# VectorE's share of the softmax exponentials: four weighted bit readings instead of five

## The chip, the cores and the metric

The kernel runs on one core of a Trainium2 chip. The core's engines work side by side, each on its own instruction queue in order: TensorE (PE, matmuls; its weight loads are listed as PEld), VectorE (DVE), ScalarE (ACT), GpSimd (POOL) and SyncE (SP, which issues most DMAs). The metric is the device time of one execution in microseconds (us), as the median over runs.

## The reference

One transformer block with adaptive layer norm: 2048 tokens, width 512, 32 heads of 16, hidden width 1376.

```python
mod = (silu(c) @ w_mod).reshape(1, 6, 1, -1)      # sa, ca, ga, sb, cb, gb
h = layernorm(x) * (1 + ca) + sa
q, k, v = split(h @ wqkv)                          # 32 heads of 16
p = softmax(einsum('bhqd,bhkd->bhqk', q, k) * 16 ** -0.5)
x = x + ga * (einsum('bhqk,bhkd->bhqd', p, v) @ wo)
h = layernorm(x) * (1 + cb) + sb
x = x + gb * (gelu(h @ w1 + b1) @ w2 + b2)
```

## The kernel before

Attention is cut into 32 *runs*. A run is one block of 512 queries (`QB`) with four heads (in the last block: half the queries with eight heads), and passes over 16 key tiles of 128 keys (`NT`). A *unit* is 128 keys by 512 score columns; a run has 16 x 4 of them, the kernel 2048.

**Scores.** TensorE computes units by `qk` (L868). The four heads sit on four strips of 32 rows, so that several small score matmuls run side by side. For ScalarE, three and two units in turn go into one PSUM tile `st` (`SPAN = (3, 2)`); `qk_a` then issues one exp over 1536 or 1024 columns (L918), written as bf16 `pt`. For VectorE, units go one at a time into `ax`, a ring of two PSUM banks that all projections and the feed-forward part use too.

**Exponentials on VectorE.** Q is scaled so that a score plus a constant, rounded to a 16-bit integer, read as bf16 bits, is near the exponential; its error depends on the place within the mantissa. `qk_d` makes such readings `ph` (L966, one instruction of 128x512 per unit, four per key tile). Then `shifts` adds constants to the integers, which moves the reading to another place of the mantissa, and the sum over all readings evens the error out. The shifts are `PH_SH = (0, 24, 46, 70, 104)`:

- one shift of 128x2048 inside `ph` gives the second reading (L1019);
- one of 128x4096 from both readings into `sh` gives the third and fourth (L1019 again, out `sh`);
- the last, into `sl`, is made by `last_shift`: VectorE writes the first columns (L998), GpSimd the rest in parts of 128 32-bit words (256 columns, L1004) by adding the tile `step`. There are up to `PMAX` = 4 parts; `LIMIT` bounds how many may be outstanding.

**The sum with V.** `pv_op` (L1060) multiplies a tile of exponentials with V and accumulates into `od`: four matmuls of 512 columns side by side (eight of 256 in the last block). V lies in `VEB` with a column of ones per head, whose product is the softmax denominator. A key tile of ScalarE takes one such pass, one of VectorE five. `normalise` then copies `od` to `OD` (L1085), sends the denominators through DRAM, and GpSimd multiplies (L1112).

**What sets the order.** At build time a planner (`Plan`) lays out every instruction: each `op` has an engine, a duration, dependencies and a priority, buffers are `Res` rings, and the planner commits whichever can start first in its own clock. `SEEDS` mixes a small random term into the priorities, one number for each 12.5 us. `DKS` names the key tiles per run that VectorE may take (`d_job` decides whether there is time; the first run has only tile 14), and `next_tile` gives back to ScalarE those that VectorE did not reach. `after_dve` and the kind `beside` hold GpSimd's parts behind chosen VectorE instructions, and `in_turn` keeps the shifts of a run behind those of earlier runs. `heat` puts in zero matmuls (L444, L449, L460) where TensorE would idle long. `layer_norm` takes its statistics tile in the operation `ln`; `make_v` projects V and copies it from `ax` to `VEB`; `v_init` lets GpSimd set the ones and zeros of `VEB`. SyncE loads x by `load_x` and the weights in slices by `load_cols` (L527).

The feed-forward part and the output projections of earlier blocks are worked in between the runs; after the last exp, the second half of the last block remains.

Of the kernel before, what the change touches and what calls it, by code (L numbers as in the profile page):

```python
# [22 lines left out]

PH_SH = (0, 24, 46, 70, 104)
NPH = len(PH_SH)


def _gain():  # L30
    tot = 0.0
    for f in range(128):
        got = 0.0
        for sh in PH_SH:
            n, m = divmod(f + sh, 128)
            got += 2.0 ** n * (1 + m / 128)
        tot += math.log2(got) - f / 128
    return tot / 128

# [12 lines left out]
DL = 0.13  # L52
# [1 line left out]
AL = 0.31  # L54
FILL = 1.6
SPREAD = 0.3
SEEDS = (819, 778, 494, 247, 422, 169, 145, 549, 366, 204, 590, 973, 619, 101, 262, 478, 482, 0, 377, 943, 929, 5, 154, 378, 13, 70, 683, 7, 419, 919, 269, 223, 66, 0, 130, 0, 185, 0, 125, 986, 361, 514, 243, 995, 230, 969, 0, 765, 158, 613, 439, 598, 14, 562, 398, 933, 223, 842, 0, 0, 579, 0, 0, 0, 0, 0)
HEAT = 1.45


# [193 lines left out]
def kernel(  # L254
# [28 lines left out]
    EPS = 1e-5  # L283
    QSC = 0.25 * 128.0 / math.log(2.0)
    ESC = math.log(2.0) / 128.0
    DKS = (2, 6, 10, 14)
    WIDE = 1
    NPT = 4
    FEW = 1
# [26 lines left out]
    r_pt = [res(f"pt{n}_", NPT, [P, n * QB], BF16) for n in SPAN]  # L316
    r_ph = res("ph", 3, [P, 2 * 4 * QB], I16)
    r_sh = res("sh", 2, [P, 2 * 4 * QB], I16)
    r_s4 = res("sl", 2, [P, 4 * QB], I16)
    r_xb = res("xb", 2, [P, TPB, D], BF16)  # L320
    r_blk = res("blk", NQ, [P, NC, D], BF16)
    r_w = res("w", 3, [P, NC, D], BF16)
# [160 lines left out]
    b1_bf = const.tile([P, NF], BF16, name="b1_bf")  # L483
    b1c = const.tile([P, NF], FP32, name="b1c")
    VEB = [keep.tile([P, TPB, 32 * VW + 15], BF16, name=f"VEB{b}") for b in range(NQ)]
    kT = [[keep.tile([P, QB], BF16, name=f"kT{cc}_{b}") for b in range(NQ)] for cc in range(NC)]

    def v_tile(t):
# [64 lines left out]
    o_mask = op("DVE", mask, 0.6, (o_io,), prio=0.0)  # L553

    step = const.tile([P, STEP_N], I32, name="step")
    o_step = op("POOL", lambda o: nc.gpsimd.memset(step, PH_SH[-1] * 65537), 0.2, prio=0.3)

    o_v0 = {}

# [4 lines left out]
                mybir.DependencyClass.Sync, mybir.DependencyReason.DATA), reason="memsets behind the first norm")  # L564
            first_ln.append(got)

    def v_init(v, prio, gate, late):
        x = v[..., 0:32 * VW].rearrange("p t (h w) -> p t h w", w=VW)
        return [op("POOL", lambda o, to=to, c=c: fill(to, c, late), 0.35, prio=prio, gate=gate)
                for to, c in ((v[..., 32 * VW:32 * VW + 15], 0.0), (x[:, :, 8:32:8, 0:15], 0.0), (x[..., 16:17], 1.0))]  # L570

    first_ln = []
    for b in range(NQ):
        late = (lambda: True) if b == 0 else (lambda: first_ln)
        o_v0[b] = v_init(VEB[b], 1.0 + b, late, b > 0)

    o_ce = op("ACT", lambda o: nc.scalar.activation(out=ce, in_=c_bf, func=ACT.Tanh, scale=0.5),
              1.5, (o_c,), prio=0.0)
# [81 lines left out]
    def layer_norm(src, deps, mod, mod_dep, hold_z, alloc_h, engines, ps_res, kind, prio,  # L660
                   after=None, nt=TPB, by_part=False):

        ln = op("NIL", None, 0.0, (), lat=0.0, prio=0.0, acq=r_ln)
        st = [op("DVE", lambda o, t=t: stats(ln, t, src(t)), 0.83, (deps[t], ln, after and after[t]), prio=prio)
              for t in range(nt)]
        rs = [op("POOL", lambda o, i=i: rstd(ln, 2 * i, 2 * i + 2), 1.3,
# [127 lines left out]
    def make_v(b, cc, kind, acq, eng, after=None):  # L794
        def vt(ps, t):
            for j in range(NC):
                nc.tensor.matmul(out=ps[:, t * P:(t + 1) * P],
                                 lhsT=o_h[b].tile[:, j, t * P:(t + 1) * P],
                                 rhs=o_w[2].tile[:, j, cc * P:(cc + 1) * P],
                                 start=(j == 0), stop=(j == NC - 1))  # L800
        mm = chain([(lambda ps, t=t: vt(ps, t), 4 * 0.071) for t in range(TPB)],
                   [(o_w1 if cc else o_w0)[2], after] + o_hd[b], kind, acq, (o_h[b], o_w[2]))

        def ev(o):
            dst = VEB[b][:, :, 8 * cc * VW:8 * (cc + 1) * VW].rearrange(
                "p t (h w) -> p t h w", w=VW)
            copy(eng, dst[:, :, :, 0:16], mm.tile[:, 0:QB].rearrange("p (t h d) -> p t h d", t=TPB, h=8))
        got = [op(eng, ev, 0.6, [mm] + o_v0[b], prio=0.3, rel=(mm,))]
        o_v[(cc, b)] = got


# [119 lines left out]
    def qk_d():  # L931
        r, kts, rows = at["D"]
        if not rows:
            r, n = d_job()
            if n == 0:
                return
            kts = [shared[r].pop(0) for _ in range(n)]
            rows = [0, 1, 2, 3]
            at["D"][:] = r, kts, rows
            o_ph[0] = op("NIL", None, 0.0, (), lat=0.0, prio=0.0, acq=r_ph)  # L940
            o_ph[0].uses += 1
            d_e[:] = [[]]
        ph = o_ph[0]
        live["D"] += 1
        k = len(d_e) - 1
        kt = kts[k]
        deps, qm = qk_deps(r, kt)
        last = len(rows) == 1

        def go(o):  # L950
            n_d[0] += 1
            rows.remove(o.row)
            if last and k + 1 < len(kts):
                rows.extend((0, 1, 2, 3))
                d_e.append([])
            qk(o, 0, r, kt, o.row)
            live["D"] -= 1
        o = op("PE", go, MM, deps + [ph], lat=PEL, mode=("qk", rows[0]), kind="qkD", acq=r_ax, rel=(qm,),
               gate=lambda: n_d[0] - n_d[1] < 2)
        o.rows = list(rows)  # L960

        def ex(e):
            n_d[1] += 1
            units[0] += 1
            c0 = (4 * k + o.row) * QB
            nc.vector.tensor_scalar(out=ph.tile[:, c0:c0 + QB], in0=o.tile, scalar1=PH_B,  # L966
                                    scalar2=0.0, op0=ALU.add, op1=ALU.max)
        e = op("DVE", ex, 0.6, (o,), lat=DL, prio=0.5, rel=(o,))
        e.run = r
        d_e[k].append(e)  # L970
        if last:
            pv_op(r, kt, d_e[k], bits(ph, k), (ph,))
            if k + 1 == len(kts):
                shifts(r, kts, ph, [e for es in d_e for e in es])
                ph.uses -= 1
# [14 lines left out]
        sh.fn = go  # L990
        return sh

    def last_shift(r, kt, first, es, acq):
        into = in_turn(op("NIL", None, 0.0, es, lat=0.0, prio=0.0, acq=acq), r)
        n = max(0, min(PMAX, LIMIT - backlog[0]))
        w = 2 * STEP_N
        cols = 4 * QB - n * w
        parts = [in_turn(op("DVE", lambda o: nc.vector.tensor_scalar(  # L998
            out=into.tile[:, 0:cols], in0=first.tile[:, 0:cols], scalar1=PH_SH[-1], scalar2=None,
            op0=ALU.add), 0.06 + 0.54 * cols / (4 * QB), [into] + es, lat=DL, prio=2.0, rel=(first,), port=True), r)]  # L1000
        for i in range(n):
            def go(o, c=slice(cols + i * w, cols + (i + 1) * w)):
                backlog[0] -= 1
                after_dve(nc.gpsimd.tensor_tensor(  # L1004
                    out=into.tile[:, c].bitcast(I32), in0=first.tile[:, c].bitcast(I32), in1=step, op=ALU.add))
            backlog[0] += 1
            parts.append(op("POOL", go, POOL_US, [into, o_step] + es, lat=0.1, prio=0.6, kind="beside", rel=(first,),
                            port=True, gate=lambda: plan.beside(POOL_MIN)))
        pv_op(r, kt, parts, bits(into, 0), (into,))
    d_e = []  # L1010

    def bits(o, k):
        return lambda: [o.tile[:, h * QB:(h + 1) * QB].bitcast(BF16) for h in range(4 * k, 4 * k + 4)]

    def shifts(r, kts, first, es):
        kt, n = kts[0], 4 * QB

        def add(j, dst, src, us, deps, acq=None):
            o = op("DVE", lambda o: nc.vector.tensor_scalar(  # L1019
                out=dst(o), in0=src(), scalar1=PH_SH[j], scalar2=None, op0=ALU.add),  # L1020
                us, deps, lat=DL, prio=2.0, acq=acq, rel=(first,), port=True)
            return in_turn(o, r)
        one = op("NIL", None, 0.0, es, lat=0.0, prio=0.0)
        a = add(1, lambda o: first.tile[:, n:2 * n], lambda: first.tile[:, 0:n], 0.6, [one])
        b = add(2, lambda o: o.tile, lambda: first.tile, 1.14, [a], r_sh)
        first.uses += 1
        pv_op(r, kt, (a,), bits(first, 1), (first,))
        first.uses -= 1
        pv_op(r, kt, (b,), bits(b, 0), (b,))
        pv_op(r, kt, (b,), bits(b, 1), (b,))  # L1030
        last_shift(r, kt, first, [one], r_s4)

    def pv_op(r, kt, deps, srcs, owners):
        cc, par, hb = run_heads(r)

        def go(o):
# [18 lines left out]
            for n, p in enumerate(parts):  # L1055
                for i in range(4):
                    c0 = VW * (8 * cc + 2 * i + p)
                    w = QB if hb is None else HB
                    at = n * HB
                    nc.tensor.matmul(out=o_od[r].tile[32 * i:32 * i + 32, n * HB:n * HB + w],  # L1060
                                     lhsT=v_tile(kt)[:, c0:c0 + 32],
                                     rhs=got[i][:, at:at + w], start=first and hb is None,
                                     stop=(left[r] == 0 and p == parts[-1]), tile_position=(0, 32 * i))
            if o.extra:
# [510 lines left out]
```

## Time and profile before

| | |
|---|---|
| median of 3 runs | 777.62 us (777.03 to 778.87) |
| the profiled execution: span | 776.9 us |
| its own time beside the span | not listed apart; the runs lie 0.1 to 2.0 above the span, their median 0.7 |
| busy: ScalarE, TensorE, VectorE, GpSimd | 749.9, 729.5, 718.4, 281.7 us |
| first exp starts, last exp ends | 16.07, 752.72 us from the span's start |
| exps on ScalarE (L918) | 312 of 128x1536, 312 of 128x1024 |
| readings made by VectorE (L966) | 488, which is 122 key tiles |
| granted TensorE clock | 0.998 of full speed in the mean |

The span is the time from the first to the last instruction of one profiled execution. A row of a group gives line, engine, operation, output and input tiles with shapes, and the count; behind the first bar the busy time and the mean duration in ns of one; behind the second the engine's idle time just ahead of the group and what ended most of it. Neighbouring instructions of an engine overlap, so busy time is less than count times mean.

### The profile page before, as it was taken

Reading aid. Unit: us, or ns where it says so; the run is one execution under the profiler, and the core shown is the slowest. Engines: PE = TensorE matmul, PEld = TensorE weight load, DVE = VectorE, ACT = ScalarE, POOL = GpSimd, SP = SyncE. Lnnn points to the kernel's source line nnn. Section 1 sums busy time; section 2 is a strip of 40 time slices with the busy share of each in tenths; the row PEclk is TensorE's granted clock in tenths of the full one; section 3 lists DMA queues with packets and bytes.
Section 4 is the critical chain, followed back from the end, with each engine's and each line's share of the span. In section 5 each row is a group of like instructions: output and inputs, shape, how many; then the busy total and the mean of one; then the engine's idle time right before and its main releaser. Section 6 shows DMA issues by size and latency. Waiting matters only on the chain.

```text
span 776.9 us, 20734 instructions
## 1 busy us (share of the span) xinstructions
PE 729.5 (94%) x8318; PEld 274.2 (35%) x8318; DVE 718.4 (92%) x1196; ACT 749.9 (97%) x683; POOL 281.7 (36%) x624
## 2 busy tenths in 40 slices
PE   8889999999999999999998999999999999999998
PEld 3433333333333223223322333323243444344454
DVE  5858899999999999999999999999999999899984
ACT  3999999999999999999999999999999999999994
POOL 6124323444443434454444433333332333223320
PEclk9999999999999999999999999999999999999999
DMA  7034000100012010000100101000111000100100
GB/s 217 30 121 109 18 24 21 35 22 18 19 36 61 22 46 24 19 9 19 44 27 15 30 13 30 18 25 24 39 51 27 18 19 18 44 19 25 53 18 28
DMA packets 39075, 28.23 MB, mean 36 GB/s; under 512 B 17958, under 2 KB 34375, under 8 KB 38979
## 3 DMA queue, kind: packets, MB, share of 16 engines
q1 hardware_dynamic: 38970, 26.91, 12.4%
q8 instruction: 65, 1.06, 0.6%
q14 instruction: 32, 0.25, 0.1%
q10 hardware_dynamic: 8, 0.00, 0.0%
HBM read 21.30 MB, written 2.61 MB: 31 GB/s over the span
## 4 chain that ended last, share of the span: by engine, by line
ACT 53%; PE 24%; DVE 11%; issue 9%; DMA 1%; POOL 1%; SPq 0%; DVEq 0%; ACTq 0%
ACT pt L918 51%; PE od L1060 8%; PE st L868 6%; DVE ph L966 6%; PE ax L1283 2%; DVE sh L1019 1%; PE ax L868 1%; PE t L1227 1%; PE ax L747 1%; DVE ph L1019 1%; PE ax L1227 1%; DMA blk<-in_w_mod_dram 1%; PE t L1412 1%; DVE OD L1085 1%; ACT g L1298 1%
## 5 line engine op out<-in xcount | busy, mean ns | idle before, releaser
L918 ACT ACTIVATE pt<-st 128x1536 bf16<-128x1536 f32 x624 | 707.9, 1429 | 3.0 <-PE st L868 1.9
L966 DVE TENSOR_SCALAR ph<-ax 128x512 int16<-128x512 f32 x488 | 320.5, 682 | 18.6 <-PE ax L868 16.4
L1004 POOL TENSOR_TENSOR sl<-ph,step 128x128 int32<-128x128 int32 x361 | 166.2, 463 | 325.0 <-DVE sh L1019 95.8
L868 PE MATMUL st<-qm,kT 32*128 32x512 bf16 x1560 | 244.0, 382 | 32.0 <-ACT pt L918 25.7
L868 PEld LDWEIGHTS <-kT 32*128 32x128 bf16 x2048 | 86.4, 91 | 248.7 <-issue 238.2
L868 PE MATMUL ax<-qm,kT 32*128 32x512 bf16 x488 | 162.2, 381 | 3.1 <-DVE ph L966 2.4
L1060 PEld LDWEIGHTS <-VEB 128*32 128x32 bf16 x5024 | 109.1, 96 | 144.7 <-issue 120.4
L1019 DVE TENSOR_SCALAR sh<-ph 128x4096 int16<-128x4096 int16 x122 | 148.2, 1216 | 1.5 <-PE od L1060 1.4
L1060 PE MATMUL od<-pt,VEB 128*32 128x512 bf16 (+1 forms) x1944 | 147.2, 342 | 0.6 <-DVE OD L1085 0.4
L1060 PE MATMUL od<-ph,VEB 128*32 128x512 bf16 (+1 forms) x1232 | 91.2, 339 | 1.2 <-DVE OD L1085 0.6
L1060 PE MATMUL od<-sh,VEB 128*32 128x512 bf16 (+1 forms) x1232 | 86.8, 340 | 0.7 <-DVE sh L1019 0.6
L1019 DVE TENSOR_SCALAR ph<-ph 128x2048 int16<-128x2048 int16 x122 | 83.2, 685 | 0.4
L998 DVE TENSOR_SCALAR sl<-ph 128x1024 int16<-128x1024 int16 (+4 forms) x122 | 59.0, 488 | 0.7 <-PE od L1060 0.4
L1112 POOL TENSOR_TENSOR OT<-OD,RB 128x128 bf16<-128x128 f32 x76 | 34.3, 456 | 62.7 <-DVE sh L1019 27.0
L1060 PE MATMUL od<-sl,VEB 128*32 128x512 bf16 (+1 forms) x616 | 48.8, 339 | 0.3 <-POOL sl L1004 0.3
L1283 PE MATMUL ax<-blk,W 128*128 128x512 bf16 (+1 forms) x176 | 43.8, 356 | 0.7 <-DVE g L1287 0.4
L1112 POOL TENSOR_TENSOR OS<-OD,RB 128x128 bf16<-128x128 f32 x48 | 21.8, 456 | 40.3 <-DVE sh L1019 14.8
L747 PE MATMUL ax<-blk,w 128*128 128x512 bf16 x116 | 33.4, 382 | 1.0 <-DMA w<-in_A_wqkv_dram 0.7
L1227 PE MATMUL ax<-w,g 128*128 128x512 bf16 x96 | 26.6, 383 | 0.0
L1287 DVE TENSOR_SCALAR g<-ax,b1c 128x512 bf16<-128x512 f32 x33 | 24.4, 743 | 1.2 <-PE ax L1283 1.2
L627 DVE BATCH_NORM_STATS2 ln_s<-xb 128x6 f32<-128x512 bf16 x32 | 21.6, 674 | 3.4 <-DMA xb<-in_A_x_dram 3.3
L1085 DVE COPY OD<-od 128x512 f32<-128x512 f32 x31 | 21.2, 683 | 3.7 <-PE od L1060 3.3
(122 smaller groups left out, 414.3 us busy)
## 6 DMA issues: line engine op xcount, KB each, us to landing
RB<-rn SPq DMA_DIRECT2D x124, 64.0 KB
xb<-in_A_x_dram SPq DMA_DIRECT2D x8, 512.0 KB
out_dram<-o SPq DMA_DIRECT2D x16, 128.0 KB
qm<-qs SPq DMA_DIRECT2D x120, 16.0 KB
W<-in_B_w_dram SPq DMA_DIRECT2D x1, 1376.0 KB
w<-in_A_wqkv_dram SPq DMA_DIRECT2D x3, 384.0 KB
blk<-in_w_mod_dram SPq DMA_DIRECT2D x2, 512.0 KB
xb<-in_w_mod_dram SPq DMA_DIRECT2D x2, 512.0 KB
```

The lines of the kernel that those rows point to most:

```text
L747: return chain([(lambda ps, j=j, n=n: nc.tensor.matmul(out=ps[:, 0:QB], lhsT=w.tile[:, j, cc * P:(cc + 1) * P], rhs=o_h[b].tile[:, j, :], ...
L868: nc.tensor.matmul(out=o.tile[:, k * QB:(k + 1) * QB], lhsT=kT[cc][kb][rows, ko * P:(ko + 1) * P], rhs=qm.tile[rows, par, :] if hb is None ...
L918: nc.scalar.activation(out=e.tile[:, 0:len(got) * QB], in_=o.tile[:, 0:len(got) * QB], func=ACT.Exp, scale=ESC)
L966: nc.vector.tensor_scalar(out=ph.tile[:, c0:c0 + QB], in0=o.tile, scalar1=PH_B, scalar2=0.0, op0=ALU.add, op1=ALU.max)
L998: parts = [in_turn(op("DVE", lambda o: nc.vector.tensor_scalar(out=into.tile[:, 0:cols], in0=first.tile[:, 0:cols], scalar1=PH_SH[-1], sca ...
L1004: after_dve(nc.gpsimd.tensor_tensor(out=into.tile[:, c].bitcast(I32), in0=first.tile[:, c].bitcast(I32), in1=step, op=ALU.add))
L1019: o = op("DVE", lambda o: nc.vector.tensor_scalar(out=dst(o), in0=src(), scalar1=PH_SH[j], scalar2=None, op0=ALU.add), us, deps, lat=DL, p ...
L1060: nc.tensor.matmul(out=o_od[r].tile[32 * i:32 * i + 32, n * HB:n * HB + w], lhsT=v_tile(kt)[:, c0:c0 + 32], rhs=got[i][:, at:at + w], star ...
L1085: OD = op("DVE", lambda o: nc.vector.tensor_copy(out=o.tile, in_=od.tile), 0.6, (last,), lat=0.3, prio=0.0, acq=r_OD, rel=(od,))
L1112: two = beside(lambda c: nc.gpsimd.tensor_tensor(out=OT.tile[:, c], in0=OD.tile[:, c], in1=o5.tile[:, c], op=ALU.mult), (OT,), (OD, o5))
L1227: nc.tensor.matmul(out=ps, lhsT=g[:, f, col:col + P], rhs=rhs, start=(f == 0), stop=(f == NF - 1))
L1283: mm = chain([(lambda ps, f=f, j=j: nc.tensor.matmul(out=ps[:, 0:N], lhsT=W1[:, j, f * P:(f + 1) * P], rhs=h.tile[:, j, 0:N], start=(j == ...
```

## The change

Four readings take the place of five. The shifts become 0, -32, 64 and 32; the two of 64 and 32 are multiplied with a copy of V scaled by 181/256, ones included, so that the sum is again near a multiple of the exponential. The copies lie in a new tile `VWB`, one slice for each tile of `DKS`, filled by VectorE in `make_v` from the same `ax` bank as `VEB`. The second reading is made inside `ph` as before. One shift by 64 of both readings gives the third and fourth in `sh`; its last columns, up to four parts of 256, are made by GpSimd from the unshifted reading with a step of 32. The tile `sl` and the function `last_shift` go. The pass of the last reading waits for VectorE's piece and all of GpSimd's parts. `DKS` has five tiles. The least reading is held at 32 instead of 0, so that -32 leaves no negative integer. The first norms take their statistics tiles in a given order, and `SEEDS` is another list.

```diff
-PH_SH = (0, 24, 46, 70, 104)
+PH_SH = (0, -32, 64, 32)
+PH_V = 181 / 256
+PH_W = (1.0, 1.0, PH_V, PH_V)
...
-        for sh in PH_SH:
+        for sh, w in zip(PH_SH, PH_W):
             n, m = divmod(f + sh, 128)
-            got += 2.0 ** n * (1 + m / 128)
+            got += w * 2.0 ** n * (1 + m / 128)
...
-    DKS = (2, 6, 10, 14)
+    DKS = (2, 5, 8, 11, 14)
...
-    r_s4 = res("sl", 2, [P, 4 * QB], I16)
...
+    VWB = keep.tile([P, len(DKS), 32 * VW + 15], BF16, name="VWB")
...
-    o_step = op("POOL", lambda o: nc.gpsimd.memset(step, PH_SH[-1] * 65537), 0.2, prio=0.3)
+    o_step = op("POOL", lambda o: nc.gpsimd.memset(step, PH_SH[3] * 65537), 0.2, prio=0.3)
...
+    o_vw0 = v_init(VWB, 5.0, lambda: first_ln, True, PH_V)
...
-        ln = op("NIL", None, 0.0, (), lat=0.0, prio=0.0, acq=r_ln)
+        ln = op("NIL", None, 0.0, (), lat=0.0, prio=int(kind[2:]) - 5.0 if kind[:2] == "in" else 0.0, acq=r_ln)
...
+        for n, kt in enumerate(DKS):
+            if kt // TPB == b:
+                def weighted(o, n=n, t=kt % TPB):
+                    dst = VWB[:, n, 8 * cc * VW:8 * (cc + 1) * VW].rearrange("p (h w) -> p h w", w=VW)
+                    nc.vector.tensor_scalar(
+                        out=dst[:, :, 0:16], in0=mm.tile[:, t * P:(t + 1) * P].rearrange("p (h d) -> p h d", h=8),
+                        scalar1=PH_V, scalar2=None, op0=ALU.mult)
+                got.append(op("DVE", weighted, 0.26, [mm] + o_vw0, prio=0.31, rel=(mm,)))
...
-                                    scalar2=0.0, op0=ALU.add, op1=ALU.max)
+                                    scalar2=-PH_SH[1], op0=ALU.add, op1=ALU.max)
...
     def shifts(r, kts, first, es):
+        kt, n, w = kts[0], 4 * QB, 2 * STEP_N
         one = op("NIL", None, 0.0, es, lat=0.0, prio=0.0)
-        a = add(1, lambda o: first.tile[:, n:2 * n], lambda: first.tile[:, 0:n], 0.6, [one])
-        b = add(2, lambda o: o.tile, lambda: first.tile, 1.14, [a], r_sh)
+        a = in_turn(op("DVE", lambda o: nc.vector.tensor_scalar(
+            out=first.tile[:, n:2 * n], in0=first.tile[:, 0:n], scalar1=PH_SH[1], scalar2=None, op0=ALU.add),
+            0.6, [one], lat=DL, prio=2.0, rel=(first,), port=True), r)
...
-        pv_op(r, kt, (b,), bits(b, 0), (b,))
-        pv_op(r, kt, (b,), bits(b, 1), (b,))
-        last_shift(r, kt, first, [one], r_s4)
+        into = in_turn(op("NIL", None, 0.0, [one], lat=0.0, prio=0.0, acq=r_sh), r)
+        m = max(0, min(PMAX, LIMIT - backlog[0]))
+        cols = 2 * n - m * w
+        b = in_turn(op("DVE", lambda o: nc.vector.tensor_scalar(
+            out=into.tile[:, 0:cols], in0=first.tile[:, 0:cols], scalar1=PH_SH[2], scalar2=None,
+            op0=ALU.add), 0.06 + 1.08 * cols / (2 * n), [into, a], lat=DL, prio=2.0, rel=(first,), port=True), r)
+        parts = [b]
+        for i in range(m):
+            def go(o, at=cols + i * w):
+                backlog[0] -= 1
+                after_dve(nc.gpsimd.tensor_tensor(
+                    out=into.tile[:, at:at + w].bitcast(I32), in0=first.tile[:, at - n:at - n + w].bitcast(I32),
+                    in1=step, op=ALU.add))
+            backlog[0] += 1
+            parts.append(op("POOL", go, POOL_US, [into, o_step, one], lat=0.1, prio=0.6, kind="beside", rel=(first,),
+                            port=True, gate=lambda: plan.beside(POOL_MIN)))
+        pv_op(r, kt, (b,), bits(into, 0), (into,), True)
+        pv_op(r, kt, parts, bits(into, 1), (into,), True)
...
-                                     lhsT=v_tile(kt)[:, c0:c0 + 32],
+                                     lhsT=(VWB[:, DKS.index(kt), c0:c0 + 32] if weighted
+                                           else v_tile(kt)[:, c0:c0 + 32]),
```

## The prediction

> **What bounds the kernel now.** I read the engine totals first, then the chain that ended last, then the costliest groups.
>
> ```profile
> span 776.9 us, 20734 instructions
> ...
> PE 729.5 (94%) x8318; PEld 274.2 (35%) x8318; DVE 718.4 (92%) x1196; ACT 749.9 (97%) x683; POOL 281.7 (36%) x624
> ...
> ACT 53%; PE 24%; DVE 11%; issue 9%; DMA 1%; POOL 1%; SPq 0%; DVEq 0%; ACTq 0%
> ...
> L918 ACT ACTIVATE pt<-st 128x1536 bf16<-128x1536 f32 x624 | 707.9, 1429 | 3.0 <-PE st L868 1.9
> L966 DVE TENSOR_SCALAR ph<-ax 128x512 int16<-128x512 f32 x488 | 320.5, 682 | 18.6 <-PE ax L868 16.4
> L1004 POOL TENSOR_TENSOR sl<-ph,step 128x128 int32<-128x128 int32 x361 | 166.2, 463 | 325.0 <-DVE sh L1019 95.8
> ```
>
> Three engines are above 90%, so shares alone decide nothing; the idle column does. ScalarE's 624 exps (L918) fill 707.9 us, with 3.0 us idle ahead of them in all. Then the waits (engine, line, waited for, us in total, times, longest), and one steady stretch of the windows (busy us of PE, PEld, DVE, ACT, POOL):
>
> ```profile
> PE st L868 <- ACT pt L918: 25.7, 79, 1.3
> ...
> PE od L1060 <- DVE sh L1019: 0.6, 2, 0.4
> ...
> PE od L1060 <- POOL sl L1004: 0.3, 1, 0.3
> ```
>
> ```profile
> 200.00:300.00 100.00, 93.19 (x1012) 31.49 (x1013) 97.93 (x153) 100.00 (x90) 40.79 (x92) 1.00 0.12 34
> ```
>
> TensorE waits for ScalarE to free a score bank (25.7 us), hardly ever for a shifted reading; ScalarE is 100% busy, VectorE 97.9%, TensorE 93.2%. So the number of exps on ScalarE sets the time, with VectorE close behind.
>
> **The change, part by part.** Counts come from the built order of both kernels, durations from the groups by shape, from one line's instructions (min/median/max) and from the timeline (start, us):
>
> ```profile
> L918 ACT ACTIVATE pt<-st 128x1536 bf16<-128x1536 f32 x312 | 512.2, 1642 | 2.3 <-PE st L868 1.9 <-PE ax L868 0.2
> L918 ACT ACTIVATE pt<-st 128x1024 bf16<-128x1024 f32 x312 | 379.5, 1216 | 0.7 <-PE ax L868 0.6
> ...
> L1019 DVE TENSOR_SCALAR ph<-ph 128x2048 int16<-128x2048 int16 x122 | 83.2, 685 | 0.4
> ```
>
> ```profile
> L1019 DVE TENSOR_SCALAR sh<-ph x122: 1157/1216/1455, 46.1 to 747.8; 128x4096 int16<-128x4096 int16 x122
> ```
>
> ```profile
> 734.53 18.18 ACT L918 ACTIVATE pt<-st 128x1536 bf16<-128x1536 f32 x16 [0.18 <-PE ax L868]
> ```
>
> ```profile
> 21.07 0.62 PE L1060 MATMUL od<-pt,VEB 128*32 128x512 bf16 x8
> ...
> 22.16 0.40 PE L1060 MATMUL od<-pt,VEB 128*32 128x512 bf16 x4
> ```
>
> *ScalarE.* VectorE's key tiles rise from 122 to 131 (not to the 156 that five a run would allow), so 36 of 1560 score units of 512 columns leave ScalarE. By the mean, 707.9/1560 = 0.454 us a unit: 16.3 us. By instructions: neighbours overlap by some 0.31 us, so 16 exps without a gap take (18.18 - 0.31)/8 = 2.234 a pair, and with 1642 - 1216 = 426 ns between the two shapes that is 1.33 and 0.90. Seven wide and eight narrow ones go, one of 512 comes (some 0.48): 9.3 + 7.2 - 0.5 = 16.0. I take **16.2 us off the path**. ScalarE's gelus, table loads and casts keep their number.
>
> *VectorE.* Evictions: 36 x 0.682 = +24.6. The pass over 4096 columns and the last pass (59.0 us in all) become one pass of 3072, 3328, 3584 or 3840 columns (56, 26, 34, 15 times). On the line between 0.685 us at 2048 columns and 1.216 at 4096 these take 0.95, 1.02, 1.08, 1.15: 134 us, with 131 x 0.685 = 90 for the other shift 224, against 148.2 + 83.2 + 59.0 = 290. The 20 weighted copies of V (128x128 from PSUM) have no row; the nearest are 0.24 (128x16), 0.33 (L651, 128x128 of bf16) and 0.48 (128x256): 4.8 to 9.6 us, 6.6 taken, the row of equal size. Sum 24.6 - 66 + 6.6 = -35. It lies beside ScalarE and counts for nothing; VectorE ends near 684 of 761 us. Each copy also holds one of two `ax` banks 0.33 us longer, with the next score or projection behind it: 0 to 6.6 us, 0 taken, as nothing on ScalarE waits for `ax` at once.
>
> *TensorE.* The passes over V lose 264 matmuls of 512 columns and 232 of 256. Four run side by side, 0.62 - 0.40 = 0.22 us per four, half for 256: 14.5 + 6.4 = 21 less. The 36 moved scores go singly instead of in twos and threes: 0 to +8. 72 more small zero matmuls (+4) and 21 fewer wide ones (-5) keep the clock up. Net 14 to 22 less under ScalarE's 16: it stays just behind.
>
> *GpSimd.* 24 more parts x 0.463 = +11 us at 36% busy, and three memsets in the front. The new wait: the last half of `sh` waits for these parts, as `sl` did. Queued behind on TensorE are the next scores, and behind them ScalarE. Before, that cost 0.3 us in all; bounds per tile are 0 and one part, 0.463. I take the near end, the row of the same wait.
>
> *The shared port.* The widest shift took 1216 ns at the median and at most 1455, with 361 GpSimd parts about: a collision cost at most 0.24 us, so 0 is taken. The Trainium skill (SBUF — State Buffer, Who interferes with whom) says that a VectorE operation in a two-port mode and a GpSimd one exclude each other, the loser blocked for a whole instruction. By that rule the 385 parts cost up to 385 x 0.463 = 178 us of VectorE and the sum would be 684 + 178 = 862; the trace shows no shift stretched by a whole part.
>
> *Front and tail.* SP now issues three 128-column slices of wqkv ahead of the second 512 KB of x. The K projection, which waited 0.69 us for its slice, finds it there; x lands some 0.85 us later (256 KB at this stretch's 300 GB/s), and its norm, whose slots the new `prio` orders, feeds the seventh exp. 0, bounds -1.2 and +1. Behind the last exp (752.7) the same work remains: 24.2 us, +-1.
>
> *Short gaps.* From the first exp (16.07) to the end of the last (752.72) are 736.7 us; 312 pairs fill 697, gelus with table loads 22, casts and modulations 5; 12 are gaps. The rewritten order has its own; nearest row is this kernel's own, bounds 6 and 21, 13 taken.
>
> Sum against the profiled span: 776.9 - 16.2 + 1 = 761.7. The runs' median (777.62) lies 0.7 above the span, so **762.4 us**. A difference of 0.2% (1.6 us) is about what a measurement of this kernel can tell from none.
>
> **Rivals.**
>
> 1. *Partly given back* (0.15): late GpSimd halves hold TensorE for one part in one tile of eight: 16 x 0.463 = 7.6 us. For it: TensorE takes work in order and is 93% busy. Against: 0.3 us before. 770.
>
> 2. *Better* (0.11): a lighter TensorE fills the banks earlier and the gaps fall to 6 us: 755.
>
> 3. *Slower, waiting for GpSimd* (0.05): the last half of `sh` is late in every tile. It decides from (16.2 + 1.6)/131 = 0.136 us a tile; at half a part, 131 x 0.23 = 30: 792. For it: GpSimd stood idle 325 us, so its parts start only behind VectorE's work. Against: that wait starts them in time, and there are two `sh` buffers.
>
> 4. *Slower, by the port* (0.02): parts fall on shifts. VectorE has 761 - 684 = 77 us of room and needs 18 more: (77 + 18)/0.463 = 205 of 385 parts would each block a shift whole. With 240, 111 - 77 = 34: 796. Against: 1455 ns at most.
>
> 5. *The clock* (0.02): a lighter TensorE lets it drop more often. The windows show one drop, behind the third gelu:
>
> ```profile
> 670.00:682.50 12.50, 12.38 (x137) 4.74 (x136) 10.62 (x17) 11.38 (x9) 4.93 (x11) 0.86 0.10 34
> ```
>
> A granted 0.86 over 12.5 us is 1.75 us of clock lost. One at each of three gelus: 3.5 more, 766. The Trainium skill (TensorE: Matmul & The Clock Gate, Part 1) halves the clock after an idle window of about 3.4 us; by it half of 3.4, 1.7 us, would be lost, and the row agrees.
>
> That the change does not do what it says holds only for "five": the built order has 131 tiles, and those are costed.
>
> **How the numbers follow.** Forecast 0.63, rivals 0.15, 0.11, 0.05, 0.02, 0.02, and 0.02 for a saving that just vanishes. Faster 0.63 + 0.15 + 0.11 + 0.02 = 0.91; same 0.02; slower 0.07. The forecast alone spans 757 to 768 (front, tail and gaps together); the range takes in nearly all of rivals 1 and 2: 756 to 771.
>
> **What would show it.** Right: 610 exps filling some 692 us with a few us idle; VectorE near 684; TensorE waiting under 2 us for GpSimd's `sh`, and most for score banks. Wrong: ScalarE idle for TensorE by tens of us, `od` waiting over 10 us for GpSimd, or shifts of 3072 columns far above 0.95 us.

## The result, and the profile after

The changed kernel takes 765.29 us (median of 4 runs, 762.14 to 768.07) beside 778.14 us for the kernel before in the same comparison: a ratio of 0.984, with a 95% interval of 0.981 to 0.987. It is faster by 12.9 us, where the prediction said 15.2.

From the page of the profiled execution after: the span, the engine totals, the TensorE clock in 40 slices, the chain by engine, and the groups that answer to those shown of before.

```profile
span 760.0 us, 19784 instructions
...
PE 700.6 (92%) x7810; PEld 260.3 (34%) x7873; DVE 690.6 (91%) x1148; ACT 734.1 (97%) x669; POOL 294.5 (39%) x651
...
PEclk9999999999899999999999999999999999999999
...
ACT 42%; PE 35%; DVE 12%; issue 9%; POOL 2%; DVEq 0%; POOLq 0%; ACTq 0%
...
L929 ACT ACTIVATE pt<-st 128x1536 bf16<-128x1536 f32 x610 | 691.9, 1379 | 4.4 <-PE st L879 2.9
L977 DVE TENSOR_SCALAR ph<-ax 128x512 int16<-128x512 f32 x524 | 343.7, 683 | 29.8 <-PE ax L879 27.3
L1028 POOL TENSOR_TENSOR sh<-ph,step 128x128 int32<-128x128 int32 x385 | 176.3, 460 | 305.9 <-DVE ph L1012 92.7
```

The exps (L918 before, L929 now) went from 707.9 to 691.9 us with 4.4 us idle ahead of them. In the chain, ScalarE's share fell from 53% to 42% and TensorE's rose from 24% to 35%: the end is now handed from engine to engine more often. TensorE's 700.6 us is too low: the page counts 7810 matmuls (PE) beside 7873 weight loads (PEld), so 63 matmul records are missing, where the page of before has 8318 of each. Two variants below with all 7873 records show 707 to 708 us. The clock line has an 8, from the stretch behind 196 us. The waits (engine, line, waited for, us in total, times, longest) name the same bottleneck as before, and the new wait for GpSimd's part of `sh` is nearly nothing:

```profile
PE st L879 <- ACT pt L929: 28.2, 82, 0.8
DVE ph L977 <- PE ax L879: 27.3, 50, 1.7
```

```profile
L1064 PE MATMUL od<-sh,VWB 128*32 128x512 bf16 (+1 forms) x1312 | 96.8, 341 | 2.2 <-POOL sh L1028 0.8
```

To see where the time went I split each profiled span by ScalarE's own instructions: the start of the first exp; the exps at the cost they have without a gap (1.33, 0.904 and 0.478 us for 1536, 1024 and 512 columns; from the start of one wide or narrow exp to the next it is 1.33 and 0.904 us at the median in both kernels); the gaps between neighbouring exps beyond that; gelus, table loads and the rest among them (about 29 us in every kernel here); and what comes behind the last exp.

| kernel | span | first exp | exps without gaps | gaps | behind the last | granted clock |
|---|---|---|---|---|---|---|
| before | 776.9 | 16.1 | 697.0 | 10.8 | 24.1 | 0.998 |
| after | 760.0 | 13.4 | 680.9 | 12.2 | 23.8 | 0.993 |
| after, again | 762.6 | 14.0 | 680.9 | 14.2 | 23.8 | 0.988 |

The exps give 16.1 us, the number the prediction was built on; the front gives 2.1 to 2.6 and the gaps take 1.4 to 3.4.

What is left is the spread. Ten runs of the changed kernel (four here, six below) lie between 762.14 and 769.4 us, and their spans follow the granted clock: 760.0 us at 0.993, 762.6 at 0.989, 767.3 at 0.982. A straight line through the ten gives 756.7 us at full clock and 0.56 us for each 0.001 of clock (correlation 0.88); one through the 45 runs of the kernel before that the experiments brought along gives 774.4 us and 0.54. The mean clock was 0.9983 before and is 0.9882 now. By these lines the kernels lie 17.7 us apart at full clock (774.4 - 756.7; an extrapolation, as none of the ten was granted more than 0.993). With the clock that is lower by 0.0101 go some 5.5 us, which leaves the 12 measured. Whether the clock takes that time or only marks slower runs is asked below. In the trace, three windows of the changed kernel (busy us of PE, PEld, DVE, ACT, POOL, then the clock) show what happens to ScalarE where the clock falls:

```profile
115.00:126.00 11.00, 10.31 (x105) 3.22 (x104) 10.88 (x19) 11.00 (x11) 6.00 (x14) 1.00 0.17 51
126.00:134.00 8.00, 7.56 (x80) 2.38 (x76) 6.83 (x13) 7.06 (x7) 1.88 (x5) 0.79 0.10 34
196.00:208.00 12.00, 11.22 (x93) 2.58 (x93) 10.51 (x16) 11.30 (x11) 4.43 (x10) 0.72 0.02 3
```

At full clock ScalarE is busy all 11 us. At 0.79 it is idle 0.94 us of 8, at 0.72 it is idle 0.70 of 12. Its idle times lie late in the stretches of half clock or just behind them (before its starts at 131.09, 204.05 and 206.85 us; half clock from 128.0 to 131.4 and from 199.7 to 206.5).

### The profile page after: what moved, and what is told of

It is laid out like the page before. It is cut to its first block, busy times and chain, and to the rows that moved or that the text cites. A ratio compares the mean times of both kernels' runs of the same rounds, so it can differ in the third digit from the quotient of the medians.

```text
span 760.0 us, 19784 instructions
## 1 busy us (share of the span) xinstructions
PE 700.6 (92%) x7810; PEld 260.3 (34%) x7873; DVE 690.6 (91%) x1148; ACT 734.1 (97%) x669; POOL 294.5 (39%) x651
## 4 chain that ended last, share of the span: by engine, by line
ACT 42%; PE 35%; DVE 12%; issue 9%; POOL 2%; DVEq 0%; POOLq 0%; ACTq 0%
ACT pt L929 41%; PE od L1064 11%; PE st L879 10%; DVE ph L977 6%; PE ax L879 3%; PE ax L1288 2%; PE ax L1232 2%; DVE sh L1021 2%; PE t L1232 1%; DVE ph L1012 1%; PE ax L750 1%; DVE OD L1090 1%; PE t L1417 1%; DVE xb L1275 1%; DVE ln_s L630 1%
## 5 line engine op out<-in xcount | busy, mean ns | idle before, releaser
L929 ACT ACTIVATE pt<-st 128x1536 bf16<-128x1536 f32 x610 | 691.9, 1379 | 4.4 <-PE st L879 2.9
L977 DVE TENSOR_SCALAR ph<-ax 128x512 int16<-128x512 f32 x524 | 343.7, 683 | 29.8 <-PE ax L879 27.3
L1028 POOL TENSOR_TENSOR sh<-ph,step 128x128 int32<-128x128 int32 x385 | 176.3, 460 | 305.9 <-DVE ph L1012 92.7
L879 PE MATMUL st<-qm,kT 32*128 32x512 bf16 x1524 | 239.4, 384 | 33.4 <-ACT pt L929 28.2
L879 PE MATMUL ax<-qm,kT 32*128 32x512 bf16 x524 | 174.2, 381 | 5.7 <-DVE ph L977 3.8
L879 PEld LDWEIGHTS <-kT 32*128 32x128 bf16 x2048 | 82.0, 91 | 240.1 <-issue 231.0
L1021 DVE TENSOR_SCALAR sh<-ph 128x3072 int16<-128x3072 int16 (+3 forms) x131 | 133.9, 1024 | 1.0
L1064 PEld LDWEIGHTS <-VEB 128*32 128x32 bf16 x3216 | 74.3, 96 | 110.7 <-issue 97.2
L1064 PE MATMUL od<-sh,VWB 128*32 128x512 bf16 (+1 forms) x1312 | 96.8, 341 | 2.2 <-POOL sh L1028 0.8
L1012 DVE TENSOR_SCALAR ph<-ph 128x2048 int16<-128x2048 int16 x131 | 90.4, 692 | 1.0
L1064 PEld LDWEIGHTS <-VWB 128*32 128x32 bf16 x1312 | 32.6, 96 | 40.6 <-issue 34.7
L1288 PEld LDWEIGHTS <-W 128*128 128x128 bf16 x176 | 13.8, 97 | 19.8 <-issue 13.2
## 6 DMA issues: line engine op xcount, KB each, us to landing
out_dram<-o SPq DMA_DIRECT2D x16, 128.0 KB
```

Source lines behind the costliest of these rows:

```text
L879: nc.tensor.matmul(out=o.tile[:, k * QB:(k + 1) * QB], lhsT=kT[cc][kb][rows, ko * P:(ko + 1) * P], rhs=qm.tile[rows, par, :] if hb is None ...
L929: nc.scalar.activation(out=e.tile[:, 0:len(got) * QB], in_=o.tile[:, 0:len(got) * QB], func=ACT.Exp, scale=ESC)
L1012: a = in_turn(op("DVE", lambda o: nc.vector.tensor_scalar(out=first.tile[:, n:2 * n], in0=first.tile[:, 0:n], scalar1=PH_SH[1], scalar2=No ...
L1021: b = in_turn(op("DVE", lambda o: nc.vector.tensor_scalar(out=into.tile[:, 0:cols], in0=first.tile[:, 0:cols], scalar1=PH_SH[2], scalar2=None,
L1028: after_dve(nc.gpsimd.tensor_tensor(out=into.tile[:, at:at + w].bitcast(I32), in0=first.tile[:, at - n:at - n + w].bitcast(I32), in1=step, ...
L1288: mm = chain([(lambda ps, f=f, j=j: nc.tensor.matmul(out=ps[:, 0:N], lhsT=W1[:, j, f * P:(f + 1) * P], rhs=h.tile[:, j, 0:N], start=(j == ...
```

## Experiments: which engine sets the time

Theory A: the number of exps on ScalarE sets the end, the other engines have room. Rivals: VectorE, or TensorE with its clock, is just as much the bound. The first set adds some 17 us of idle work to one engine at a time, in the changed kernel, with the order of everything else as it was.

**The changed kernel again.**

> The changed kernel once more, beside which the other three of this set are read. All theories: 762 to 768 us a run, the median near 765, run time 2.1 us above the span.

Measured: 764.72 us (763.61 to 769.4), ratio to before 0.9855 (0.9831 to 0.9878). The run time is 2.1 us above the span in every run.

**Fifteen exps twice.**

```diff
-            nc.scalar.activation(out=e.tile[:, 0:len(got) * QB], ...
+            twice[0] += 1
+            for _ in range(2 if twice[0] % 41 == 20 else 1):
+                nc.scalar.activation(out=e.tile[:, 0:len(got) * QB], ...
```

> The changed kernel with 15 of its 610 wide or narrow exps issued twice in a row, same input and same output, nothing else moved: about 15 x 1.38 = 20 us more of ScalarE when all are wide, 16 to 20 us as they fall. Theory A (the count of ScalarE's exps sets the end): the time rises by nearly all of that, to 779 to 786 us, and the gaps between exps stay near 12 us. Rival VectorE (it has become a second bound at 691 us busy): less than half arrives, under 774 us, since ScalarE would have had time to spare. Rival TensorE or its clock: under 770 us.

Measured: 787.54 us (784.63 to 788.66), 22.8 more than the changed kernel beside it. Seven wide and eight narrow exps were doubled, 16.6 us without gaps. So more than all of it arrives, 1.5 us above theory A's range, at a granted clock of 0.974 to 0.985 in the five runs.

**Every fifth first shift twice.**

```diff
-        a = in_turn(op("DVE", lambda o: nc.vector.tensor_scalar(...)
+        def second(o):
+            twice[0] += 1
+            for _ in range(2 if twice[0] % 5 == 1 else 1):
+                nc.vector.tensor_scalar(...)
+        a = in_turn(op("DVE", second, ...
```

> The changed kernel with every fifth 2048-column shift on VectorE issued twice (27 more, 27 x 0.60 to 0.69 = 16 to 19 us of VectorE). Theory A: 0 to 4 us more, since VectorE has some 70 us of idle time and waits for score banks; the added time comes out of its 30 us of waiting for score banks. Rival VectorE: 12 to 19 us more, 777 to 784 us, with ScalarE waiting for score banks that VectorE holds up.

Measured: 777.53 us (772.85 to 780.76), 12.8 more. Theory A is wrong here by its own numbers. The page and the waits of this kernel:

```profile
PE 707.8 (91%) x7810; PEld 257.5 (33%) x7873; DVE 706.9 (91%) x1175; ACT 738.2 (95%) x669; POOL 294.1 (38%) x651
...
L929 ACT ACTIVATE pt<-st 128x1536 bf16<-128x1536 f32 x610 | 696.0, 1313 | 16.6 <-PE st L879 8.5
```

```profile
DVE ph L977 <- PE ax L879: 27.7, 51, 2.3
...
ACT pt L929 <- PE st L879: 8.5, 16, 2.0
```

```profile
PE ax L879 <- DVE ph L977: 6.5, 23, 0.5
PE od L1069 <- DVE ph L1017: 5.0, 11, 0.8
```

```profile
PE od L1069 <- DVE sh L1026: 3.3, 8, 0.9
```

VectorE has 16.3 us more work and just as much idle time as in the changed kernel: its wait for scores in `ax` was 27.3 us and is 27.7. The added work did not go into the idle time; it lengthened the span. Who lost time is ScalarE, whose idle time ahead of exps rose from 4.4 to 16.6 us, and between them stands TensorE: its waits for evictions and shifts (the last three rows) come to 14.8 us, where the same three come to 5.4 in the changed kernel (3.8, 1.1 and 0.5). TensorE works in order, so while a score matmul or a pass waits for VectorE, ScalarE's next scores stand behind it.

**Eighty groups of zeros on TensorE.**

```diff
-            if o.extra:
+            passes[0] += 1
+            if o.extra or left[r] > 1 and passes[0] % 11 == 5:
                 zeros(r)
```

> The changed kernel with 80 more groups of four matmuls of zeros, each added to a sum and changing nothing in it, after passes of the weighted sum (80 x 0.22 = 17.6 us of TensorE). Theory A: 0 to +3 us, as TensorE waits 28 us for exps to free score banks. Rival TensorE: +10 to +18 us. Rival clock (the half-clock stretches of 3.4 and 6.8 us at 128 and 200 us come from too little matmul work in the array and hold up ScalarE): the added matmuls remove some of the drops, the granted clock rises from 0.99 and the time falls by 0 to 3 us.

Measured: 771.07 us (765.71 to 772.62), 6.3 more for 17.6 us of work, at clocks of 0.984 to 0.997. TensorE does not carry all, nor is it free.

The second set takes work away.

**Exps cut short.**

```diff
+            e.less = count[0] % 30 == 15
+            w = QB if e.less else len(got) * QB
-            nc.scalar.activation(out=e.tile[:, 0:len(got) * QB], in_=o.tile[:, 0:len(got) * QB],
+            nc.scalar.activation(out=e.tile[:, 0:w], in_=o.tile[:, 0:w],
...
-                pv_op(r, kt, es, lambda src=src: [x.tile[:, m * QB:(m + 1) * QB] for x, m in src], es)
+                pv_op(r, kt, es, lambda src=src: [x.tile[:, 0:QB] if x.less else x.tile[:, m * QB:(m + 1) * QB] for x, m in src], es)
```

> The changed kernel with 20 of its three-unit exps cut to one unit of 512 columns (its two other units are not computed, the weighted sum reads the first one three times); 20 x 0.85 = 17 us of ScalarE taken away, nothing else moved. After the doubled work of the last set (16.5 us on ScalarE cost about 20, 17 us on VectorE about 12, 17.6 us on TensorE about 6) two readings stand. Theory A (ScalarE's work sets the end, the other two engines wait for it): 10 to 17 us less, 748 to 755 us. Rival B (three engines in step: the others, at 91 to 92 per cent, take over as soon as ScalarE is lighter): 2 to 8 us less, 757 to 763 us.

Measured: 759.19 us (756.98 to 759.42), ratio to before 0.9758 (0.9737 to 0.9778): 5.5 us less than the changed kernel by the medians, 7.5 by the ratios, for 17 us taken away. By the split, the exps without gaps fell from 680.9 to 663.9 us and the gaps rose from 12.2 to 26.2. ScalarE's row says what it waits for:

```profile
L934 ACT ACTIVATE pt<-st 128x1536 bf16<-128x1536 f32 x610 | 678.5, 1297 | 14.5 <-PE ax L879 7.4 <-PE st L879 6.0
```

ScalarE now waits for scores, 7.4 us of it for scores that stand behind those of VectorE.

**Shifts cut short.**

```diff
+        count[0] += 1
+        less = count[0] % 2
+        some = n if less else cols
...
-            out=into.tile[:, 0:cols], in0=first.tile[:, 0:cols], ...
+            out=into.tile[:, 0:some], in0=first.tile[:, 0:some], ...
-        pv_op(r, kt, parts, bits(into, 1), (into,), True)
+        pv_op(r, kt, parts, bits(into, 0 if less else 1), (into,), True)
```

> The changed kernel with every second shift to the third and fourth reading cut to its first 2048 columns (the fourth reading's VectorE share is not made there, and its pass reads the third reading once more); 22 us of VectorE taken away, GpSimd's parts and everything else unchanged. Theory A: 0 to 3 us less, 762 to 765 us, as ScalarE still has its 681 us of exps. Rival B: 5 to 12 us less, since taking work off VectorE would be worth as much as adding it costs.

Measured: 763.29 us (759.64 to 764.0), ratio 0.9803 (0.978 to 0.9827): 1 to 4 us less, which is theory A's number and not rival B's 5 to 12. VectorE's busy time fell by 17.5 us to 673.1, and the gaps between exps are 12.9 us:

```profile
PE 707.4 (93%) x7873; PEld 260.9 (34%) x7873; DVE 673.1 (88%) x1148; ACT 733.8 (96%) x669; POOL 292.7 (38%) x651
```

So the pair of experiments on VectorE is lopsided: 16 us more cost 12.8, 17.5 us less bring almost nothing. It is not a bound by itself, but it has no room either.

| kernel | us (median) | first exp | exps without gaps | gaps | granted clock of the profiled run |
|---|---|---|---|---|---|
| 15 exps twice | 787.54 | 13.6 | 697.5 | 18.3 | 0.985 |
| 27 shifts twice | 777.53 | 13.8 | 680.9 | 28.7 | 0.984 |
| 80 groups of zeros | 771.07 | 14.1 | 680.9 | 20.6 | 0.988 |
| 20 exps cut | 759.19 | 13.7 | 663.9 | 26.2 | 0.991 |
| half the shifts cut | 763.29 | 13.9 | 680.9 | 12.9 | 0.991 |
| GpSimd's parts on VectorE (below) | 775.92 | 14.0 | 680.9 | 28.5 | 0.978 |

The clocks differ, so I also read each kernel's line of span over clock at one clock, 0.985. Against the changed kernel there, the exps twice cost 17.6 us for 16.6 of work, the shifts twice 11.2 for 16.3, the zeros 4.9 for 17.6. So the doubled exps arrive whole and little more; the rest of their 22.8 us goes with the lower clock.

What stands after this lies between A and B: ScalarE's exps are the floor, and the gaps on top of them come from VectorE and TensorE, which run in step with it. Theory A holds for added exps, and for taking exps away only as far as the other two can follow. Rival B's claim for VectorE, that its work is worth as much taken away as added, does not hold.

**GpSimd's parts left to VectorE.**

```diff
-            out=into.tile[:, 0:cols], in0=first.tile[:, 0:cols], ...
+            out=into.tile[:, 0:2 * n], in0=first.tile[:, 0:2 * n], ...
...
-                after_dve(nc.gpsimd.tensor_tensor(...))
```

> The changed kernel with GpSimd's 385 parts left out and VectorE's second shift always making all 4096 columns, in the same order: 385 x 256 columns x 0.26 ns = 25.7 us more on VectorE, 177 us less on GpSimd, no waits for GpSimd's parts. From the shifts issued twice (12 us for 17) theory B (three engines in step) gives 15 to 20 us more, 780 to 785 us, and the shift's own rate of 0.26 ns a column unchanged (no shared-port cost). Rival port (GpSimd beside VectorE slows its shifts): the shifts get faster per column than in the changed kernel and less than 10 us is lost.

Measured: 775.92 us (772.21 to 780.72), ratio 0.9986 (0.9962 to 1.001). Without GpSimd's parts the kernel takes what the kernel before takes: the parts are worth 11 us, less than the 15 to 20 expected (7.3 us by the two lines at a clock of 0.985). One line's instructions (duration min/median/max) show the shift's rate without the parts:

```profile
L1021 DVE TENSOR_SCALAR sh<-ph x131: 1164/1219/1303, 48.3 to 742.3; 128x4096 int16<-128x4096 int16 x131
```

With no GpSimd part about, a shift of 4096 columns takes 1219 ns at the median; before, with 361 parts about, it took 1216. The changed kernel's shifts by shape lie on the same line, 947, 1031, 1087 and 1152 ns:

```profile
L1021 DVE TENSOR_SCALAR sh<-ph 128x3072 int16<-128x3072 int16 x56 | 53.1, 947 | 0.4
L1021 DVE TENSOR_SCALAR sh<-ph 128x3584 int16<-128x3584 int16 x34 | 37.0, 1087 | 0.3
L1021 DVE TENSOR_SCALAR sh<-ph 128x3328 int16<-128x3328 int16 x26 | 26.8, 1031 | 0.1
L1021 DVE TENSOR_SCALAR sh<-ph 128x3840 int16<-128x3840 int16 x15 | 17.3, 1152 | 0.2
```

At the median the parts cost VectorE nothing. That does not make a collision free: the plan keeps the parts off the shifts. In the changed kernel 128 of the parts' 177 us lie over evictions, and only 15 of the 385 parts lie over a shift by more than 0.05 us. Where the two meet, one of them is stretched. This part began 0.03 us into a shift and took 1450 ns in place of the median 455; the shift kept its length (start, us):

```profile
65.13 1.15 DVE L1021 TENSOR_SCALAR sh<-ph 128x3840 int16<-128x3840 int16 x1
65.16 1.45 POOL L1028 TENSOR_TENSOR sh<-ph,step 128x128 int32<-128x128 int32 x1 [3.09 <-DVE o L1212]
...
66.66 0.40 PE L1064 MATMUL od<-sh,VWB 128*32 128x512 bf16 x4 [0.85 <-POOL sh L1028]
```

The other way round, three shifts of 2048 columns that began 0.14 us into a part took 858 to 864 ns, where the median is 682. By the rule of the Trainium skill (SBUF — State Buffer, Who interferes with whom) a blocked shift would be a whole part, 0.46 us, longer. The late part agrees with the rule: it ended 0.33 us behind the shift. The late shifts are 0.18 us longer, less than the 0.31 us that the parts still had to run, so they were not held back whole.

## Experiments: the clock

Each half-clock stretch in the traces lasts 3.41 us or a multiple, and the stretches of one execution begin on one grid of that step. For each step of the grid I summed what the array did: each matmul's columns at 2.4 a nanosecond (the trace shows 216 ns from one full matmul of 512 columns to the next), counted where it starts, times the share of the array's rows and columns that it uses (a score matmul uses 32 of 128 rows, a quarter). In the eleven executions of the changed kernel and its variants with this plan, between 20 and 730 us, 33 steps with a share below 0.34 were followed by half clock and 4 were not. The other 17 of the 50 steps followed by half clock had shares from 0.34 to 0.42, where most steps were not; no step above 0.43 was. Busy time alone separates them worse: of the 50 steps with the lowest share 35 were followed by half clock, of the 50 with the least busy time 20. The step before the drop at 199.7 us (share 0.31) and the next two windows, TensorE alone:

```profile
196.30:199.71 3.41, 2.81 (x24) 0.99 0.00 0
199.71:206.54 6.83, 6.65 (x45) 0.50 0.02 5
206.54:209.95 3.41, 3.41 (x48) 1.00 0.02 2
```

TensorE was busy 2.81 of the 3.41 us ahead of the drop, 2.19 of them with scores (L879). The Trainium skill (TensorE: Matmul & The Clock Gate, Part 1) has the clock halved after an idle window of about 3.4 us; the length agrees, idleness does not, as this step was not idle. The next three kernels add zeros where the share is low.

**18 and 35 groups behind the scores.**

```diff
             live["A"] -= 1
+            added()
...
+    def added():
+        spot[1] += heat_at.get(spot[0], 0)
+        spot[0] += 1
+        while spot[1] and pv_run[0] is not None and left[pv_run[0]] > 0:
+            zeros(pv_run[0])
+            spot[1] -= 1
```

> The changed kernel with 18 groups of four matmuls of zeros (added to a sum, changing nothing; 18 x 0.22 = 3.9 us of TensorE) put in right after those score matmuls around which the trace of the changed kernel has under 0.34 of the array in use over 3.41 us, score matmuls counted at a quarter since they use 32 of the 128 rows. Clock theory (the clock is halved for 3.41 us after a stretch of too little use of the array): the granted clock rises from 0.982-0.993 to 0.995 or more in most runs, 758 to 763 us and a narrower spread. Rival (drops come from the length of waits, or at random; zeros only cost): clock unchanged and 765 to 768 us.

> The same with 35 groups (7.7 us of TensorE), wherever the use of the array is under 0.37 over 3.41 us. Clock theory: a granted clock of 0.997 or more, 758 to 763 us, little to tell from 18 groups, as the added work costs some 2 us where 80 groups cost 6. Rival: 766 to 770 us at an unchanged clock.

Measured: 766.85 us (766.55 to 767.16) at clocks of 0.990 to 0.993 with 18 groups, and 767.72 us (764.66 to 770.73) at 0.991 to 1.0 with 35. With 18 groups the clock stays below the 0.995 expected; with 35 it rises to 0.996 in the mean, three of six runs at 0.997 or more. So the clock theory's first half holds in part for 35 groups, and its second half fails: no time comes back. With 35 groups the runs still follow the clock, from 762.5 us of span at 1.0 to 768.6 at 0.991; the line has only moved up, by 5.5 us at full clock for 7.7 us of zeros. Behind the scores TensorE is just what ScalarE waits for, which would explain why most of the zeros' time counts there.

**49 groups in TensorE's idle places.**

```diff
+            fill_hole()
             for k, u in enumerate(got):
                 qk(o, k, *u)
```

> The changed kernel with 49 groups of zero matmuls (10.8 us of TensorE), each put just ahead of score matmuls before which TensorE stood idle 0.25 us or longer in both traces of the changed kernel. 18 and 35 groups behind the scores brought the granted clock to 0.991 and 0.996, but 766.9 and 767.7 us. Theory (the clock gives back some 1.3 us a drop, but there the zeros stood in TensorE's way): in the idle places they cost little, the clock is again near 0.995, and the time is 758 to 763 us. Rival (the drops cost nothing by themselves, they only mark slow stretches): 764 to 770 us whatever the clock.

Measured: 764.66 us (761.3 to 766.83) at clocks of 0.990 to 0.999, ratio 0.9844 (0.9822 to 0.9867): the changed kernel's own time and the rival's range, not the 758 to 763 expected. The zeros are cheaper here (10.8 us of them; the best run has 759.2 us of span at 0.999), and the mean clock rose from 0.988 to 0.994, yet the two cancel. That the time follows the clock within every kernel is measured; how much of it the drops cause, and how much a run that is late for another reason causes drops, these three kernels don't separate.

## Experiments: the readings or the start values

The change replaces both the readings and the list `SEEDS` that steers the planner. Both kernels with all values at 0:

```diff
-SEEDS = (0, 0, 793, 682, ...)
+SEEDS = (0,) * 66
```

> The changed kernel with all 66 drawn start values of its planner at 0: 120 key tiles on VectorE instead of 131, 1568 units and 627 exps on ScalarE. By ScalarE's units against the changed kernel: 44 x 0.454 = 20 us more, 785 us. To be read against the kernel before with its values at 0.

> The kernel before with its 66 drawn start values at 0: 114 key tiles on VectorE instead of 122, 1592 units on ScalarE, 32 x 0.454 = 14.5 us more than before, 791 us. If the gain is the readings' own, the pair at 0 differs by 24 units, 10.9 us, and some 3 us at the front; if it comes with the start values, the pair at 0 is equal within 3 us.

Measured: 788.45 us (788.27 to 794.46) and 819.89 us (818.49 to 822.16), where 785 and 791 were expected. Without drawn values the changed kernel gains 31 us, not 11: in the split, 10.7 us of exps and 20.3 of gaps (38.8 against 18.5 us). The groups of the two:

```profile
L918 ACT ACTIVATE pt<-st 128x1536 bf16<-128x1536 f32 x637 | 723.7, 1366 | 29.7 <-PE od L1060 17.1
```

```profile
L929 ACT ACTIVATE pt<-st 128x1536 bf16<-128x1536 f32 x627 | 712.4, 1370 | 10.1 <-PE od L1064 4.6
```

So the gain does not come from luckier start values: the kernel before owed 43 us to its values, the changed one 24. How much of the 31 us belongs to the readings is open: the 10.7 us of exps come with the tiles that VectorE took over, but the gaps are those of two orders, and each was run at one neutral setting only.

One part of the edit was not tried apart. The kernel before used 122 of the 125 key tiles that a list of four allows (31 runs of four, one of one), and the list of five came with the four readings. No run has five readings with the longer list or four with the shorter one. VectorE's 97.9% in the steady stretch of before speaks against much gain from the list alone, but that is not a measurement.

## Why the prediction was right

- **ScalarE, -16.2.** Measured -16.1, by the same 36 units at a cost that the trace after confirms (1.33 and 0.904 us from exp to exp); 691.9 us busy against "some 692". This step carries the result, and the doubled exps show that exps set the time.
- **The new wait, 0, and the port, 0.** The wait cost 0.8 us in one place, and the shift's median rate is the same with and without GpSimd's parts. Rivals 1 and 3, which rest on that wait, fell. Rival 4 fell because 15 parts met a shift where it needed 205, not because a collision costs nothing: the one wait of 0.8 us is itself a part that a shift held up.
- **Gaps, +1.** +1.4 in the profiled execution, at its clock of 0.993; +3.4 at 0.988.
- **Front, 0.** The first exp came 2.6 us earlier, outside the bounds of -1.2 and +1. Its start is 13.4 to 14.1 us in all later traces, and 13.7 in the kernel before with its start values at 0, so the edit in the front need not be its cause; with one trace of the kernel before, 16.1 us may be that order's or that execution's.
- **The offset, +0.7.** A run is 2.1 us longer than its span here and 1.7 to 1.9 before. The 776.9 us of the profiled execution belonged to a run near 778.7, not to the median of 777.62; two errors, the offset and the execution, met in one number and hid each other, which was luck.
- **The clock, a rival at 0.02.** Mis-sized: it was to come with the gelus at 766 us, with one drop each. The drops come in stretches of scores where little of the array is in use, and the mean clock fell by 0.010; some 5.5 us go with that by the measured lines, as cause or as mark. The forecast of 762.4 equals the changed kernel's best runs; its median is 2 to 3 us later.
- **VectorE, -35, near 684, "counts for nothing".** The groups' sum fell by 36.3 us (783.0 to 746.7), as costed: +23.2 evictions, -66.1 shifts, +5.4 copies at 0.283 each, where 6.6 was taken. But the engine's busy time fell by only 27.8, to 690.6: neighbours overlap, and the sum of groups counts the overlap twice. And the 77 us of room named with rival 4 isn't there: between 41 and 736 us VectorE is idle 46 us, and 16 us of added work left that idle time as it was.
- **TensorE, 14 to 22 less.** 28.9 less by the page (729.5 to 700.6), but 63 records are missing there. With all records, in the two kernels with work cut (707.4 and 708.1), it is 21 to 22 less, the upper end of the forecast. It didn't shorten the gaps, so rival 2 fell too.

## To carry to other kernels

Three engines above 90% in a fixed order work in step: what is taken from the busiest one arrives while the others follow, and what is added arrives whole on the busiest and in part on the others (16.6 us of exps cost 17.6 at equal clock, 16.3 of shifts 11.2, 17.6 of zeros 4.9), so idle time of an in-order engine is no room until an experiment has put work there. Make the sum against a run's own time, with its clock beside it, since two kernels can differ by several us in clock alone. When start values of a planner change together with an edit, compare both kernels with neutral values before you say what the edit is worth.

## What was not expected of the hardware

- Half clock came with TensorE busy 82% of the 3.41 us ahead of it (2.81 us), when its work was scores that use 32 of 128 rows. Weighted by the part of the array in use, 33 of the 37 steps below 0.34 were followed by half clock, and none above 0.43.
- 7.7 us of zeros brought the clock from a mean of 0.988 to 0.996, and the spans were 1.8 us longer in the mean, not shorter.
- Work of 16.6 us on the busiest engine made the kernel 22.8 us slower, and its runs were granted a clock of 0.974 to 0.985, where the changed kernel's had 0.982 to 0.993. At equal clock the work costs 17.6 us. That the longer waits lighten the array's load and so lower the clock fits the other traces, but was not tried by itself.
- A GpSimd part that began 0.03 us into a VectorE shift took 1450 ns in place of 455, and shifts that began 0.14 us into a part took some 860 in place of 682. Medians over hundreds of instructions hide this, since the plan lets the two meet in 15 cases only.
